# Holding loads back by the bytes in flight: a fused attention and feed-forward kernel

## The chip, the cores and the metric

The kernel runs on one core of a Trainium2 chip. The metric is the device time of one execution in microseconds. One core has five engines with instruction queues of their own: TensorE (PE in the profile; PEld is its weight load), VectorE (DVE), ScalarE (ACT), GpSimd (POOL) and SyncE (SP). GpSimd, SyncE and ScalarE also issue DMAs, which 16 DMA engines carry out.

## The reference

```
B, H, S, D = 8, 12, 448, 64            # q, k, v: [B, H, S, D], float32
scores = q @ k^T / sqrt(D)
attn   = relu(scores)**2 / S
x      = (attn @ v), heads side by side -> [3584, 768]
gate   = relu(x @ w_gate)              # w_gate, w_val: [768, 1536]
val    = x @ w_val
out    = (gate * val) @ w_out          # w_out: [1536, 768]; out: [3584, 768] float32
```

## The kernel before

All inputs are loaded once into SBUF and turned to bf16 by the load itself. The weights stay there: `wg`, `wv` (each 128 x 6 x 1536) and `wo`. Attention goes by quads, four heads of one batch, so there are 24 quads. A quad's k and q go to a `raw` buffer (two of them; the first six quads use space in `gvT`, which is filled with something else later), its two halves of v to a `vv` buffer (three of them; two early quads use `gvT` again). TensorE (the first six quads, L540, L547 and L588) or a copy on VectorE or ScalarE and a DMA transpose from SyncE (the later ones, L612 and L618) turn q and k round into `qkT`. Then come scores (L686), relu and square on ScalarE and VectorE (L697, L699, L709, L711), and the product with v (L728), which leaves x of the batch in `xT`.

The feed-forward part of a batch runs between the quads of later batches. The first two batches multiply with `wg` and `wv` plainly (L793); the others use a scheme with fewer multiplications (L902), and the product with `wo` uses a like one (L1017). Their prepared weights `gvT` and `woT` are made by VectorE from `wg`, `wv` and `wo` (L820, L839). TensorE also gets some filler matmuls in the first 32 us (L1171).

All this is emitted once, without loops on the chip. A planner in the kernel's own Python code merges three written-out orders (`PE_ORDER` for TensorE, `LOAD_ORDER` for the loads, `AHEAD` for VectorE, ScalarE and SyncE) with modelled durations and so fixes the order on every engine. The order on an engine is its queue: an instruction that waits holds back all behind it.

GpSimd issues 117 loads (L404) and does nothing else but four memsets at its start; only the first two pieces of q come from SyncE and ScalarE. A load waits for what its destination needs (that a `raw` or `vv` buffer's last reader is done), and for one of eight DMA semaphores, which the loads take in turn, so for the load eight places before it. Sizes as written in bf16: a q or k load is 224 KB, a v load 112 KB, 256 columns of `wg` or `wv` 384 KB, 128 columns 192 KB, a piece of `wo` 576 KB; the sources are float32, twice that.

Of the kernel before, what the change touches and what calls it, by code (L numbers as in the profile page):

```python
# [9 lines left out]
BF16 = mybir.dt.bfloat16  # L10
# [298 lines left out]
def kernel(  # L309
# [10 lines left out]
    nc = tc.nc  # L320
# [27 lines left out]
    pool = ctx.enter_context(tc.tile_pool(name="sb", bufs=1))  # L348
# [51 lines left out]
    others, pool_ops = [], []  # L400


    def dma_in(dst, src, n_desc, us, deps=(), alloc=(), share=0.25):
        op = Op({"POOL": (0.5 + 0.0004 * n_desc,) * 2}, lambda: nc.gpsimd.dma_start(out=dst(), in_=src),  # L404
                deps=deps, alloc=alloc)
        op.load, op.share = us, share
        pool_ops.append(op)
        return op
# [3 lines left out]
    def load_gv(m0, m1):  # L412

        cols = slice(m0 * 128, m1 * 128)
        for ops, sb, w in ((wg_op, wg, moe_w_gate), (wv_op, wv, moe_w_val)):
            src = w.rearrange("(kd p) f -> p kd f", p=128)
            op = dma_in(lambda sb=sb: sb[:, :, cols], src[:, :, cols], 768,
                        1.075 * (m1 - m0) + (0.0 if wv_op or sb is wv else 0.65))
            for m in range(m0, m1):
                ops[m] = op  # L420

    def load_out(par, hf):
        src = moe_w_out.rearrange("(g par p) m -> p par g m", p=128, par=2)
        wo_op[(par, hf)] = dma_in(lambda: wo[:, par, hf], src[:, par, :, hf * OH:(hf + 1) * OH], 768, 3.0, share=0.19)
# [20 lines left out]
    def first_loads(st, src):  # L445


        n = 4 * QT * D
        wide = hT.rearrange("p k s -> p (k s)").bitcast(FP32)[:, :n].rearrange("p (h t d) -> p h t d", h=4, t=QT)

        def pair(j, eng, queue):
            hs = slice(2 * j, 2 * j + 2)
            k_op = dma_in(lambda: st.raw()[64:128, hs], src(k)[:, hs], 128, 0.05)
            k_op.to = (2.05, None)[j]
            ld = Op({eng: (0.65, 0.65)}, lambda: queue.dma_start(out=wide[0:64, hs], in_=src(q, 0, QT)[:, hs]))
            ld.load, ld.share, ld.hw = 0.1, 0.25, True
            cv = Op({"DVE": (0.46, 0.55)}, lambda: nc.vector.tensor_copy(st.raw()[0:64, hs, :QT], wide[0:64, hs]), deps=[ld])
            cv.kind = "wide"
            others.extend([ld, cv])
            return [k_op, cv]  # L460

        table = Op({"ACT": (1.3, 1.3)}, lambda: None)
        st.qk_ops = [pair(0, "ACT", nc.scalar), pair(1, "SP", nc.sync)]
        table.deps.append(others[-4])
        others.append(table)
        st.load_q = lambda t0, t1: dma_in(lambda: st.raw()[0:64, :, t0:t1], src(q, t0, t1), 256, 0.17 * (t1 - t0))
# [818 lines left out]
```

## Time and profile before

| what | value |
|---|---|
| two runs | 403.55 and 410.82 us, median 407.19 |
| span of the profiled execution | 402.3 us; the nearer run, 403.55 us, is 1.2 us longer |
| TensorE, VectorE, ScalarE, GpSimd busy | 98%, 81%, 68%, 19% |
| mean granted clock of TensorE | 0.990 |
| loads from GpSimd (queue q0) | 23.50 MB, 43.1% of the 16 DMA engines' time |
| stores and transposes (queue q1) | 18.98 MB, 26.5% |
| chain that ended last | PE 95%, DMA 1%, DVE 1% |

The page divides the span into 40 slices of about 10 us and gives for each the busy tenths of every engine, the granted TensorE clock and what the DMA engines moved. The chain that ended last is followed back from the last instruction to what released each. In the view of GpSimd's instructions in order of time, a bracket behind an instruction says how long GpSimd stood idle before it and what ended that. "Landing" is the moment at which a load's semaphore shows that all of it is there.

### The profile page before, as it was taken

Reading aid. Unit: us, or ns where it says so; the run is one execution under the profiler, and the core shown is the slowest. Engines: PE = TensorE matmul, PEld = TensorE weight load, DVE = VectorE, ACT = ScalarE, POOL = GpSimd, SP = SyncE. Lnnn points to the kernel's source line nnn. Section 1 sums busy time; section 2 is a strip of 40 time slices with the busy share of each in tenths; the row PEclk is TensorE's granted clock in tenths of the full one; section 3 lists DMA queues with packets and bytes.
Section 4 is the critical chain, followed back from the end, with each engine's and each line's share of the span. In section 5 each row is a group of like instructions: output and inputs, shape, how many; then the busy total and the mean of one; then the engine's idle time right before and its main releaser. Section 6 shows DMA issues by size and latency. Waiting matters only on the chain.

```text
span 402.3 us, 8737 instructions
## 1 busy us (share of the span) xinstructions
PE 393.8 (98%) x3472; PEld 210.1 (52%) x3472; DVE 326.1 (81%) x568; ACT 274.0 (68%) x399; POOL 75.7 (19%) x121
## 2 busy tenths in 40 slices
PE   6999999999999999999999999999999999999995
PEld 3567745454455554444455554444555555555563
DVE  5688788999989879969988989888789967758662
ACT  3697786477979728969879868878788843333221
POOL 7946441020430110311030221300100000000000
PEclk9799999999999999999999999999999999999999
DMA  8999999948988995193698796682224320000245
GB/s 121 192 198 199 201 193 183 147 48 136 124 144 171 162 116 115 26 145 56 84 141 153 152 131 129 82 92 47 46 37 99 80 59 2 0 0 2 59 118 139
DMA packets 77337, 43.54 MB, mean 108 GB/s; under 512 B 40688, under 2 KB 77296, under 8 KB 77296
## 3 DMA queue, kind: packets, MB, share of 16 engines
q0 software_dynamic: 34640, 23.50, 43.1%
q1 hardware_dynamic: 42192, 18.98, 26.5%
q8 instruction: 27, 0.44, 0.5%
q10 hardware_dynamic: 464, 0.49, 0.4%
q14 instruction: 14, 0.11, 0.1%
HBM read 47.19 MB, written 11.01 MB: 145 GB/s over the span
## 4 chain that ended last, share of the span: by engine, by line
PE 95%; DMA 1%; DVE 1%; POOL 0%; issue 0%; ACT 0%; POOLq 0%
PE ps L902 36%; PE ps L1017 25%; PE ps L793 14%; PE ps L686 10%; PE ps L728 8%; DMA gvT<-in_q_dram 1%; PE ps L1171 1%; PE ps L540 1%; PE ps L588 1%; DVE at L711 1%; POOL gvT L404 0%; DVE at L699 0%; DVE qkT L515 0%; DVE f L853 0%; ACT xT L744 0%
## 5 line engine op out<-in xcount | busy, mean ns | idle before, releaser
L697 ACT ACTIVATE at<-ps 128x896 bf16<-128x896 f32 (+4 forms) x116 | 103.2, 906 | 22.6 <-PE ps L686 21.8
L849 ACT COPY f<-ps 128x448 f32<-128x448 f32 x99 | 52.1, 532 | 45.8 <-PE ps L902 34.2
L709 ACT ACTIVATE at<-at 128x896 bf16<-128x896 bf16 (+1 forms) x72 | 67.0, 947 | 2.0 <-DVE at L699 1.2
L711 DVE TENSOR_TENSOR at<-at 128x896 bf16<-128x896 bf16 (+4 forms) x99 | 58.9, 607 | 9.2 <-ACT at L697 8.1
L699 DVE TENSOR_SCALAR at<-ps 128x896 bf16<-128x896 f32 (+4 forms) x55 | 58.4, 1064 | 6.9 <-PE ps L686 6.2
L404 POOL DMA_DIRECT2D vv<-in_v_dram x44 | 26.7, 611 | 165.5 <-PE ps L686 152.5
L686 PE MATMUL ps<-qkT 64*64 64x448 bf16 (+2 forms) x756 | 51.5, 342 | 1.0 <-ACT xT L744 0.3
L902 PE MATMUL ps<-xT,gvT 128*128 128x448 bf16 x216 | 50.9, 353 | 0.0
L902 PE MATMUL ps<-sx,wv 128*128 128x448 bf16 x216 | 50.6, 353 | 0.1
L902 PE MATMUL ps<-xT,wg 128*128 128x448 bf16 x216 | 49.7, 353 | 0.0
L902 PEld LDWEIGHTS <-gvT 128*128 128x128 bf16 x324 | 30.7, 98 | 30.5 <-issue 3.2
L1017 PEld LDWEIGHTS <-sh 128*128 128x128 bf16 x312 | 29.5, 98 | 22.9 <-issue 3.6
L1017 PEld LDWEIGHTS <-hT 128*128 128x128 bf16 x270 | 25.3, 98 | 20.5 <-issue 4.5
L1017 PE MATMUL ps<-wo,hT 128*128 128x384 bf16 x192 | 35.6, 327 | 0.0
L686 PEld LDWEIGHTS <-qkT 64*64 64x64 bf16 x756 | 19.5, 106 | 27.5 <-issue 22.4
L728 PE MATMUL ps<-at,vv 64*64 64x448 bf16 (+2 forms) x700 | 33.4, 327 | 0.0
L1007 DVE SCALAR_TENSOR_TENSOR o<-ps,f 128x384 f32<-128x384 f32 x41 | 22.5, 554 | 12.1 <-PE ps L1017 7.2
L902 PEld LDWEIGHTS <-wv 128*128 128x128 bf16 x216 | 20.6, 98 | 21.0 <-issue 2.8
L793 PE MATMUL ps<-xT,wv 128*128 128x448 bf16 (+2 forms) x180 | 31.3, 316 | 0.0
L902 PEld LDWEIGHTS <-wg 128*128 128x128 bf16 x216 | 20.6, 98 | 19.9 <-issue 1.7
L851 ACT ACTIVATE f<-ps 128x384 f32<-128x384 f32 x37 | 18.2, 491 | 18.6 <-PE ps L1017 18.3
L793 PE MATMUL ps<-xT,wg 128*128 128x448 bf16 (+2 forms) x180 | 30.6, 315 | 0.0
(72 smaller groups left out, 495.5 us busy)
## 6 DMA issues: line engine op xcount, KB each, us to landing
out_dram<-o SPq DMA_DIRECT2D x108, 96.0 KB, 2.2
vv<-in_v_dram POOLq DMA_DIRECT2D x44, 112.0 KB, 5.1
raw<-in_k_dram POOLq DMA_DIRECT2D x18, 224.0 KB, 5.4
raw<-in_q_dram POOLq DMA_DIRECT2D x18, 224.0 KB, 6.0
wo<-in_moe_w_out_dram POOLq DMA_DIRECT2D x4, 576.0 KB, 16.7
wg<-in_moe_w_gate_dram POOLq DMA_DIRECT2D x5, 384.0 KB, 9.9
wv<-in_moe_w_val_dram POOLq DMA_DIRECT2D x5, 384.0 KB, 10.6
gvT<-in_k_dram POOLq DMA_DIRECT2D x5, 224.0 KB, 6.3
```

The lines of the kernel that those rows point to most:

```text
L404: op = Op({"POOL": (0.5 + 0.0004 * n_desc,) * 2}, lambda: nc.gpsimd.dma_start(out=dst(), in_=src), deps=deps, alloc=alloc)
L686: nc.tensor.matmul(banks()[64 * j:64 * j + 64, z, h2], lhsT=self.k_of(j, h2, k), rhs=self.q_of(j, h2), start=True, stop=True)
L697: nc.scalar.activation(self.at_of(i, m), banks(), AF.Relu)
L699: nc.vector.tensor_scalar_max(self.at_of(i, m), banks(), 0.0)
L709: nc.scalar.activation(a, a, AF.Square)
L711: nc.vector.tensor_tensor(a, a, a, ALU.mult)
L728: nc.tensor.matmul(ps[64 * h2:64 * h2 + 64, ps2.idx + j, :n], lhsT=st.v_of(j, h2, c), rhs=self.at_of(c)[64 * j:64 * j + 64, 0, h2], start= ...
L793: nc.tensor.matmul(ps[:, pb.idx, z * n:(z + 1) * n], lhsT=w[:, kd, fc], rhs=xT_t[xbuf[b].idx][:, kd, cols], start=(kd == 0), stop=(kd == K ...
L849: nc.scalar.copy(dst, src)
L902: nc.tensor.matmul(ps[:, pb.idx, :S], lhsT=w(g)[:, fc], rhs=rhs, start=start and g == 0, stop=stop and g == KH - 1, skip_group_check=True)
L1007: op = Op({"DVE": V384}, lambda: nc.vector.scalar_tensor_tensor(o_t[ob.idx], ps[:, pb.idx, :OH], float(out_scale), f_t[fb.idx][:, :OH], AL ...
L1017: nc.tensor.matmul(ps[:, pb.idx, :OH], lhsT=lhs(kf), rhs=rhs(kf), start=start and kf == 0, stop=kf == FH - 1, skip_group_check=True)
```

## The change

Every load looks back over the loads issued before it, newest first, and adds up their source bytes until 600,000 are reached. If a load lies behind those, and was not looked at before, GpSimd copies one element of its destination into a one-element tile `seen` ahead of issuing the new load. The copy needs the landing of that load, so GpSimd waits for it. 91 such copies stand in the program. The order of the loads, and of the work on the other engines, is the same.

```diff
+    seen = pool.tile([1, 1], BF16, name="seen")
+    issued = []
+    IN_FLIGHT = 600000
+    FLAT = {2: "a b -> a b", 3: "a b c -> a (b c)", 4: "a b c d -> a (b c d)"}
+
     def dma_in(dst, src, n_desc, us, deps=(), alloc=(), share=0.25):
-        op = Op({"POOL": (0.5 + 0.0004 * n_desc,) * 2}, lambda: nc.gpsimd.dma_start(out=dst(), in_=src),
-                deps=deps, alloc=alloc)
+        def emit():
+            d = dst()
+            size = 4
+            for n in src.shape:
+                size *= n
+            held, k = 0, len(issued)
+            while k > 0 and held < IN_FLIGHT:
+                k -= 1
+                held += issued[k][1]
+            if held >= IN_FLIGHT and k > 0 and issued[k - 1][0] is not None:
+                at = tuple(slice(0, 1) for _ in issued[k - 1][0].shape)
+                nc.gpsimd.tensor_copy(seen[0:1, 0:1], issued[k - 1][0][at].rearrange(FLAT[len(at)]))
+                issued[k - 1] = (None, issued[k - 1][1])
+            issued.append((d, size))
+            nc.gpsimd.dma_start(out=d, in_=src)
+
+        op = Op({"POOL": (0.5 + 0.0004 * n_desc,) * 2}, emit, deps=deps, alloc=alloc)
         op.load, op.share = us, share
         pool_ops.append(op)
         return op
```

## The prediction

> **What bounds the kernel now.** I read the first part of the page and its slices, then the stretches of the first 60 us, then GpSimd's own instructions in order of time, because the change touches only what GpSimd issues.
>
> ```profile
> PE 393.8 (98%) x3472; PEld 210.1 (52%) x3472; DVE 326.1 (81%) x568; ACT 274.0 (68%) x399; POOL 75.7 (19%) x121
> PEclk9799999999999999999999999999999999999999
> DMA  8999999948988995193698796682224320000245
> ```
>
> TensorE is busy for 98% of the 402.3 us, so only some 8.5 us could be won at all. The DMA row shows the second resource: for the first fifth of the span the DMA engines are as full as TensorE, and later they are not.
>
> ```profile
> 5.00:10.00 5.00, 3.37 (x67) 1.88 (x65) 2.47 (x5) 2.53 (x4) 3.71 (x7) 0.89 1.18 162
> 10.00:15.00 5.00, 5.00 (x71) 2.71 (x70) 2.79 (x6) 2.11 (x4) 4.66 (x7) 0.50 1.36 197
> 20.00:30.00 10.00, 9.46 (x177) 6.75 (x176) 8.88 (x15) 9.16 (x14) 4.56 (x7) 1.00 1.42 199
> 30.00:40.00 10.00, 9.96 (x189) 7.74 (x186) 8.12 (x14) 7.50 (x14) 5.81 (x9) 1.00 1.38 199
> 40.00:50.00 10.00, 10.00 (x136) 7.26 (x133) 7.58 (x14) 7.25 (x12) 4.97 (x8) 1.00 1.36 201
> ```
>
> After the bounds of the stretch and its length come busy times of PE, PEld, DVE, ACT and POOL, the granted clock, the DMA share and GB/s. From 20 to 50 us loads move at a steady 199 to 201 GB/s (of written bf16 bytes), while TensorE hardly idles. That is a balance: the loads arrive only just ahead of their readers.
>
> ```profile
> 18.12 1.67 POOL L404 DMA_DIRECT2D wg<-in_moe_w_gate_dram  x2
> 21.29 0.84 POOL L404 DMA_DIRECT2D wv<-in_moe_w_val_dram  x1 [0.26 <-DMA wg<-in_moe_w_gate_dram]
> 28.40 0.85 POOL L404 DMA_DIRECT2D wv<-in_moe_w_val_dram  x1 [1.38 <-DMA wg<-in_moe_w_gate_dram]
> 30.96 0.63 POOL L404 DMA_DIRECT2D gvT<-in_k_dram  x1 [1.71 <-DMA wg<-in_moe_w_gate_dram]
> ```
>
> I number the loads from 0 in the order of their issue. The program has eight semaphores for GpSimd's loads, so a load already waits for the one eight places before it. Load 31, at 30.96, waits for load 23 (the second of the pair at 18.12), which landed at 30.68: it took 11.7 us because it stood behind seven others. GpSimd restarts 0.28 us after the landing.
>
> **What the change adds.** 91 of the 117 loads get a one-element copy ahead of them. Nothing is removed, and the order on TensorE, VectorE, ScalarE and SyncE stays. On GpSimd only later loads queue behind a waiting copy, and their readers wait for them. Five VectorE instructions (four at the building of gvT and woT, one late copy at L1069) and one SyncE wait also name a copy; those copies are over long before, so I cost them at nothing. If not, one costs its own lateness once.
>
> The size counts float32 source bytes: a q or k load is 459 KB, a v load 229 KB, 256 columns of wg or wv 786 KB, a piece of wo 1180 KB. So 600 KB means one large weight load, or two of q and k, or three of v, and the next load is issued when the load before those has landed. In place of seven loads ahead there are one to three.
>
> The price of one turn, landing to next landing, has three terms:
> - waking GpSimd: 0.29 us, from the row above and its like;
> - the copy: not in this trace. Nearest rows: the four 128x1 memsets at the start follow each other every 0.03 us, and GpSimd's other kind of instruction, a load's issue, takes 0.59. I take 0.15, as it is nearer to a memset, with one read added;
> - from issue to landing, less the transfer. Load 113, a v load with nothing around it (its group lands in 2.7 us), has 0.57 of transfer, so 2.16. The very first load gives 3.27 - 0.57 = 2.7. A k load at 246.2, beside transposes, gives 4.6 - 1.15 = 3.5; from 10 to 48 us no transposes run. I take 2.3.
>
> One turn is then 0.29 + 0.15 + 2.3 = 2.74 us. Bounds: 2.16 + 0.29 + 0.03 = 2.5 and 2.7 + 0.29 + 0.59 = 3.6.
>
> Transfers, as spacings of landings in the full queue: v 0.57, q or k 1.15, 256 weight columns 1.97 us. With two weight loads in turn, two loads take 2.74 + 1.97 = 4.71 us where they took 3.94; three k loads 2.74 + 1.15 = 3.89 where they took 3.45; four v loads 3.31 where they took 2.28. The full queue becomes one with holes.
>
> Now load by load. A load is issued at its gate's landing + 0.44, or after the issue before it; it lands at max(landing before it, issue + 2.3) + its own spacing of before. Around load 26: load 21 lands at 31.36 instead of 26.15, so load 23, held by it, goes out at 31.80, can start to land at 34.10, where load 22 was done at 33.33 (a hole of 0.77), and lands at 36.66. Load 26 (wv, 128 columns) is held by 23: out at 37.10, ready at 39.40 behind load 25 at 38.41 (a hole of 0.99), landed at 41.17, where it had landed at 34.20. It is 6.97 us late; its matmuls stood at 37.95, so its slack was 3.75.
>
> Where load n lands later than the slack allows, the rest of TensorE's order is moved by the difference. The loads that set this:
> - start: loads 3 and 5, which TensorE waits for now, land at 8.93 and 11.68. Load 5 is needed at 11.72. No loss, with nothing to spare. Load 12 costs the first 0.3 us.
> - load 26: late 6.97, slack 3.75: 3.2 us in all by 38 us.
> - load 35 (wv): lands at 54.8 instead of 45.70, late 9.1, slack 3.75: 5.3 in all.
> - load 37 (wv): late 9.9, slack 4.2: 5.7 in all by 53 us.
> - loads 52 and 53 (the last piece of wo, a q load): late 13.2, slacks 5.2 and 3.7, both of VectorE, which TensorE follows at 88 us after about a microsecond of slack: 8.2 in all.
> - after 92 us GpSimd mostly waits for TensorE, and the page has 152.5 us of such waits. Bursts of three to six loads get 0.5 to 1 us later at their ends; a q load at 141 us without slack loses 0.2. In all 8.4 us.
>
> **The clock.** In the table above TensorE idled 1.6 us between 5 and 10 us, in three pieces and among short transposes, and then the granted clock was 0.50 from 8.9 to 15.7 us. New idle pieces of 2 to 3 us, at 38 and at 88 us, can do the same for 3.4 us or more, which costs half of that, 1.7 us. At 38 us the next late load would swallow it; at 88 us nothing would. I add 1 us, between 0 and 3.4. The Trainium skill (TensorE: Matmul & The Clock Gate, Part 1: The HAM clock gate) says that the clock halves after at least one idle window of about 3.4 us. By that rule no stall of my list is long enough and the term would be nothing; the row shows half speed after less.
>
> **Sum.** The lowest run shown is 403.55 us, which I take for the profiled execution: a span of 402.3 and 1.2 around it. 403.55 + 8.4 + 1.0 = 413 us. The median shown, 407.19, is that of two runs, 403.55 and 410.82, and lies 3.6 above; if the changed kernel's runs spread likewise, its median can be that much higher.
>
> **Rivals.**
> - *The slack swallows most of it.* With the turn at its floor of 2.5 us, the same working gives load 26 about 1.2 us of lateness beyond its slack and 4.3 us in all: 408 us. For it: the quiet v loads at 2.7 to 2.8 us. Against it: weight loads have three times the descriptors and a longer issue (0.85 against 0.60 us).
> - *A slow turn.* If the copy takes as long as an issue, or landing takes the 2.7 of the first load, the turn is 3.1 to 3.6 us and the working gives 14 to 23 us, the clock's share with it: 418 to 427. For it: VectorE is 75 to 90% busy beside the copies, and they are many. Against: issues of GpSimd vary by only 0.1 us beside that VectorE load.
> - *Not slower: a shorter queue lands faster.* If fewer loads in flight make each land sooner, the holes close. The place is the same 10 to 60 us; the working gives no loss at a turn of 2.1 us or less, 0.6 below mine. What could then be won is the idle time before 25 us, some 3.7 us, of which the waits for loads 0 to 5 are about half: 402 to 404 us. Against it: 2.16 from issue to landing was measured with nothing else in flight, and already exceeds 2.1. The Trainium skill (DMA: Bandwidth & Descriptors, Latency and other measured facts) has a lighter HBM load make a DMA's fixed cost smaller, which speaks for this rival; no load of the trace lands faster than the quiet 2.7 us.
> - *The hold doesn't hold*, since eight semaphores already limit the queue: then 403 to 404. Against it: loads now stand seven deep, and each copy waits for the landing of a load two to four places back.
>
> **How the numbers follow.** Forecast (6 to 13 us more) 0.50, slack 0.20, slow turn 0.22, shorter queue 0.06, no hold 0.02. The predicted time is the forecast's, 413. The range goes from 407, below the floor of the turn, to 427, its upper bound; outside are the two last rivals and the far tail. A measurement of this kernel can tell about 2%, some 8 us, from no change. Above that lie the slow turn and 0.8 of the forecast: slower 0.62. Within: the rest of the forecast, the slack and most of the last two: 0.36. Faster: 0.02.
>
> **What would show it.** Right: 91 copies on GpSimd, most of those before 90 us with idle time ahead of them that a DMA ended; loads of wg and wv landing in some 4 to 5 us instead of 10; about 160 GB/s from 20 to 50 us instead of 199 (the 38.3 us of landings from load 4 to 37 become 48); TensorE's busy time unchanged with new idle pieces near 38, 50 and 88 us, ended by DMA or by VectorE; the stretch after 100 us of the same length as before, moved by 8 to 9 us. Wrong: GB/s still near 199 (the turn is short), stalls in the first 12 us (the start has less to spare than I think), copies of 0.5 us or more, or new waits of TensorE after 100 us.

## The result, and the profile after

The changed kernel took 427.39 and 430.85 us, median 429.12, against 407.19 before: a ratio of 1.059 (95% interval 1.043 to 1.075). The ratios, here and below, are estimates from runs outside a slower state that some executions of the chip show, and so are not quite the quotients of the medians. On a second chip, with more runs, the ratio was 1.077 (1.070 to 1.084). The forecast was 413 us with a range to 427; the direction was right, the size was not. In the experiments, on four chips, 62 runs of the kernel before had a median of 403.0 us, so the 403.55 from which the sum was made is the better measure of the two that were shown.

The page's head and slices for the changed kernel:

```profile
PE 403.5 (95%) x3472; PEld 214.3 (50%) x3472; DVE 327.5 (77%) x568; ACT 274.2 (64%) x399; POOL 96.4 (23%) x212
PEclk9579698999899999999999999999999999999999
DMA  7899999999959999718768879775152320000145
```

The DMA digits go no higher than 9 (90% or more) and hide the fall; the GB/s of the stretches show it (columns as in the prediction):

```profile
10.00:20.00 10.00, 7.83 (x121) 4.58 (x117) 5.04 (x12) 4.33 (x7) 5.51 (x14) 0.50 0.87 106
20.00:50.00 30.00, 23.99 (x417) 17.66 (x419) 18.34 (x33) 18.13 (x28) 14.18 (x29) 0.84 1.04 127
```

From 20 to 50 us the loads move 127 GB/s instead of 199, and TensorE works for 24 of the 30 us. GpSimd's own instructions in order of time, from load 19 to load 21:

```profile
26.07 0.82 POOL L423 DMA_DIRECT2D wg<-in_moe_w_gate_dram  x1
29.49 0.18 POOL L420 COPY seen<-wg 1x1 bf16<-1x1 bf16 x1 [2.60 <-DMA wg<-in_moe_w_gate_dram]
29.94 0.82 POOL L423 DMA_DIRECT2D wv<-in_moe_w_val_dram  x1 [0.28 <-issue]
32.50 0.56 POOL L420 COPY seen<-wg 1x1 bf16<-1x1 bf16 x1 [1.75 <-DMA wg<-in_moe_w_gate_dram]
33.01 0.63 POOL L423 DMA_DIRECT2D gvT<-in_q_dram  x1
```

The load at 26.07 landed at 32.38, and the copy at 32.50 answers to that: GpSimd stands still while only one or two loads are under way. Mostly a copy starts 0.12 us after the landing and takes 0.18, as the first one here, and the next load begins some 0.26 us behind it: 0.56 us from landing to issue (the median over the copies that waited is 0.57). TensorE's long idle pieces, in its instructions in order of time:

```profile
47.63 1.14 PE L813 MATMUL ps<-xT,wv 128*128 128x192 bf16 x6 [3.28 <-DMA wv<-in_moe_w_val_dram]
65.67 1.12 PE L813 MATMUL ps<-xT,wv 128*128 128x448 bf16 x5 [3.63 <-DMA wv<-in_moe_w_val_dram]
71.49 1.31 PE L813 MATMUL ps<-xT,wv 128*128 128x448 bf16 x6 [1.05 <-DMA wv<-in_moe_w_val_dram]
109.40 0.38 PE L706 MATMUL ps<-qkT 64*64 64x448 bf16 x2 [1.88 <-DVE hT L823]
```

These are loads 26, 35 and 37 and the wait for VectorE that the prediction named, later than it gave. The chain that ended last says the same: DMA has 14% of the span where it had 1%.

```profile
PE 82%; DMA 14%; POOL 1%; issue 1%; DVE 1%; POOLq 0%; DVEq 0%
```

### The profile page after: what moved, and what is told of

The parts are those of the page before. It is cut to its first block, busy times and chain, and to the rows that moved or that the text cites. A ratio compares the mean times of both kernels' runs of the same rounds, so it can differ in the third digit from the quotient of the medians.

```text
span 425.4 us, 8887 instructions
## 1 busy us (share of the span) xinstructions
PE 403.5 (95%) x3472; PEld 214.3 (50%) x3472; DVE 327.5 (77%) x568; ACT 274.2 (64%) x399; POOL 96.4 (23%) x212
## 4 chain that ended last, share of the span: by engine, by line
PE 82%; DMA 14%; POOL 1%; issue 1%; DVE 1%; POOLq 0%; DVEq 0%
PE ps L922 34%; PE ps L1037 23%; PE ps L813 10%; PE ps L706 8%; PE ps L748 6%; DMA gvT<-in_q_dram 4%; DMA wv<-in_moe_w_val_dram 3%; DMA wg<-in_moe_w_gate_dram 3%; DMA vv<-in_v_dram 2%; DMA gvT<-in_k_dram 1%; DMA raw<-in_q_dram 1%; POOL seen L420 1%; DMA gvT<-in_v_dram 1%; POOL gvT L423 1%; DVE woT L859 0%
## 5 line engine op out<-in xcount | busy, mean ns | idle before, releaser
L719 DVE TENSOR_SCALAR at<-ps 128x896 bf16<-128x896 f32 (+4 forms) x55 | 58.4, 1066 | 12.3 <-PE ps L706 11.9
L706 PE MATMUL ps<-qkT 64*64 64x448 bf16 (+2 forms) x756 | 54.8, 363 | 2.1 <-DVE hT L823 1.9
L922 PEld LDWEIGHTS <-gvT 128*128 128x128 bf16 x324 | 30.7, 98 | 30.4 <-issue 3.1
L813 PE MATMUL ps<-xT,wv 128*128 128x448 bf16 (+2 forms) x180 | 33.2, 328 | 9.3 <-DMA wv<-in_moe_w_val_dram 8.7
L748 PE MATMUL ps<-at,vv 64*64 64x448 bf16 (+2 forms) x700 | 34.8, 337 | 1.1 <-DMA vv<-in_v_dram 1.1
L706 PEld LDWEIGHTS <-qkT 64*64 64x64 bf16 x756 | 20.9, 113 | 29.4 <-issue 25.2
L813 PE MATMUL ps<-xT,wg 128*128 128x448 bf16 (+2 forms) x180 | 32.4, 328 | 0.0
L922 PEld LDWEIGHTS <-wg 128*128 128x128 bf16 x216 | 20.6, 98 | 19.9 <-issue 1.7
```

Source lines behind the costliest of these rows:

```text
L706: nc.tensor.matmul(banks()[64 * j:64 * j + 64, z, h2], lhsT=self.k_of(j, h2, k), rhs=self.q_of(j, h2), start=True, stop=True)
L719: nc.vector.tensor_scalar_max(self.at_of(i, m), banks(), 0.0)
L748: nc.tensor.matmul(ps[64 * h2:64 * h2 + 64, ps2.idx + j, :n], lhsT=st.v_of(j, h2, c), rhs=self.at_of(c)[64 * j:64 * j + 64, 0, h2], start= ...
L813: nc.tensor.matmul(ps[:, pb.idx, z * n:(z + 1) * n], lhsT=w[:, kd, fc], rhs=xT_t[xbuf[b].idx][:, kd, cols], start=(kd == 0), stop=(kd == K ...
L922: nc.tensor.matmul(ps[:, pb.idx, :S], lhsT=w(g)[:, fc], rhs=rhs, start=start and g == 0, stop=stop and g == KH - 1, skip_group_check=True)
```

## The experiments

All are edits of the changed kernel. The ratios are to runs of the kernel before on the same chip.

**Which holds cost.** Three kernels keep the holds of one part of the load order only, by a condition on the load's number; the first is shown, the others have `14 <= len(issued) < 56` and `len(issued) >= 56`.

```diff
-            if held >= IN_FLIGHT and k > 0 and issued[k - 1][0] is not None:
+            if held >= IN_FLIGHT and k > 0 and issued[k - 1][0] is not None and len(issued) < 14:
```

> Holds only ahead of loads 0 to 13. My theory (the price is the length of one turn from landing to next landing, 3.3 us instead of the 2.74 that I had taken, paid where loads arrive just in time): the changed kernel's first 22 us stay as they were there, TensorE 4 to 5 us late by then, and the full queue afterwards makes nothing good: 4 to 6 us over before, 408 to 410 us. Rival A (the start and the half clock that follows it make most of the loss): 12 us or more.

> Holds only ahead of loads 14 to 55. My theory: the start is that of before; load 26 is late by 8 us against a slack of 3.75, load 37 by 18 against 4.2, load 52 by 22 against 5.2: 15 to 18 us over before, 419 to 422 us. Rival A (start): under 12 us.

> Holds only ahead of loads 56 to 116. My theory: GpSimd waits for TensorE there anyway: within 1 us of before. Rival B (every hold costs something, the late bursts too, and half of the holds are here): 5 us or more over before.

Measured: the first 14 loads 1.011 (1.007 to 1.015), some 4.4 us; loads 14 to 55 1.060 (1.055 to 1.064), some 24 us; loads 56 to 116 0.997 (0.993 to 1.001). The start costs what was expected, and rival A falls. The middle costs more than expected, by itself as much as the whole change on its first chip, though less than the 31 us of the second (below). The late holds, 52 of the 91, cost nothing that can be measured, and rival B falls: there GpSimd waits for TensorE anyway.

**The copy without its wait.** The 91 copies stand at their places but read a constant.

```diff
+    fixed = pool.tile([1, 1], BF16, name="fixed")
+    nc.gpsimd.memset(fixed, 1.0)
...
-                nc.gpsimd.tensor_copy(seen[0:1, 0:1], issued[k - 1][0][at].rearrange(FLAT[len(at)]))
+                nc.gpsimd.tensor_copy(seen[0:1, 0:1], fixed[0:1, 0:1])
```

> All 91 copies at their places, but of an element that no load writes, so none of them waits for a landing. My theory: the wait is the price, not the copy; a queue of seven loads hides 0.18 us of copy and the dispatch behind it: within 2 us of before. Rival C (the copies' own time on GpSimd is the price, 91 times 0.18 us and 0.28 us of dispatch, up to 40 of them in the first 90 us): 8 to 16 us over before.

Measured: 1.001 (0.997 to 1.004). From 20 to 50 us this kernel's loads move as much as before:

```profile
20.00:50.00 30.00, 29.93 (x494) 21.95 (x491) 24.41 (x41) 24.26 (x38) 21.33 (x41) 1.00 1.38 199
```

So 91 copies cost nothing as work of GpSimd, and rival C falls. What costs is that the next issue waits for a landing.

**The middle in two parts**, with the changed kernel once more on the same chip; the conditions are `14 <= len(issued) < 46` and `46 <= len(issued) < 56`.

> The changed kernel once more, unaltered, as the measure for the three others on this chip: 22 to 26 us over before.

> Holds only ahead of loads 14 to 45, so wg, wv, q, k and v of the middle, and none ahead of wo. My theory (turns of 3.3 us pile up lateness while the queue is the limit, and the last load short of its slack sets the loss): load 37 is some 18 to 20 us late against a slack of 4.2, and the wo loads add nothing: 13 to 17 us over before. Rival D (the loss is made among the four wo loads, where the end of the loss was seen): under 8 us.

> Holds only ahead of loads 46 to 55 (wo, and the q, k and v among them). My theory: with slacks of 5 us and a transfer of 3 us a load, the lateness stays near the slack: 0 to 3 us over before. Rival D: 8 us or more.

Measured: the changed kernel 1.077 (1.070 to 1.084), some 31 us; loads 14 to 45 1.050 (1.045 to 1.055), some 20 us; loads 46 to 55 1.001 (0.997 to 1.004). The changed kernel and the part to load 45 came out 3 to 5 us above what was expected. Rival D falls, since most of the loss is there without the wo holds. But they cost nothing only by themselves. Matmul by matmul against the trace of before, TensorE is 19.0 us late ahead of its wait at 109.40 us in the changed kernel and 23.5 us late by 115 us; in the second trace of that kernel it goes from 20.8 to 26.3 at the same place, and with the holds of loads 14 to 45 alone it stays at 17.9. So behind a queue that is late already, the wo holds add some 5 us, the half clock behind that wait included.

**The clock.** Matmuls of nothing fill TensorE's stalls ahead of loads 26, 35, 37 and of the scores near 109 us, so that it should not idle there.

```diff
+    done = {"gv": 0, "s": 0}
+    FILL = {("gv", 66): 14, ("gv", 126): 16, ("gv", 138): 5, ("s", 292): 8}
+
+    def fill_at(b, kind, n):
+        one = woT.rearrange("p a f m -> p (a f m)") if kind == "gv" else wg[:, 0]
+        for _ in range(FILL.get((kind, done[kind]), 0)):
+            nc.tensor.matmul(ps[:, b, :S], lhsT=one[:, :128], rhs=one[:, :S], start=True, stop=True)
+        done[kind] += n
...
+                fill_at(ps2.idx, "s", 4 * len(slots))
...
+                        fill_at(pb.idx, "gv", KD)
```

> The changed kernel with 14, 16, 5 and 8 matmuls of nothing put into TensorE's four long stalls (ahead of the first use of loads 26, 35 and 37, and of the scores at 109 us), some 2.6, 3.0, 0.9 and 1.5 us at full clock, so that the clock should stay at 1.0 behind them; their products are overwritten. My theory (late loads set the end, and a slow TensorE between two late loads costs nothing; only the half-speed stretch behind the last stall does): 1 to 3.5 us less than the changed kernel. Rival E (the half clock, 9.7 us of longer matmuls, is a loss of its own): 6 us or more less.

Measured: 1.069 (1.061 to 1.077) beside the 1.077 (1.070 to 1.084) of the changed kernel on the same chip, about 3 us less. The two intervals overlap, so this run does not tell the theories apart. Nor did the fill do all that it was meant to: in its trace, of the slowest of its four runs, TensorE still idles 3.96 us ahead of the scores, which now start at 116.77 us, and is at half speed from 118.0 to 121.4. What speaks against rival E are, weakly, the changed kernel's own runs on two chips: mean clocks of 0.964, 0.967, 0.967, 0.972, 0.974 and 0.980 went with 427, 431, 432, 434, 431 and 435 us. A higher clock did not go with a shorter time. The next experiment says more.

**The dose.** The limit alone is changed.

```diff
-    IN_FLIGHT = 600000
+    IN_FLIGHT = 1200000
```

> The limit at 1,200,000 instead of 600,000 bytes: two large weight loads, three of q or k or six of v ahead of a new one. My theory (a turn of 3.3 us must be covered by the transfers of the loads still in flight): two weight loads cover 3.9 us, so most holes close, and what stays is at the start and behind slow DMA engines: 1 to 8 us over before. Rival F (any hold costs, since the sixteen DMA engines drift apart by 2 to 3 us in the full queue and a hold waits for the last of them): 12 us or more over before.

> The limit at 2,400,000 bytes, three to four large loads ahead. My theory: the transfers in flight cover turn and drift, and the eight semaphores limit nearly as much: within 2 us of before. Rival F: 5 us or more over before.

Measured: 1,200,000 bytes 1.046 (1.040 to 1.053), some 19 us; 2,400,000 bytes 1.002 (0.998 to 1.006). From 20 to 50 us, the first and then the second:

```profile
20.00:50.00 30.00, 27.83 (x499) 20.88 (x494) 23.25 (x40) 22.34 (x36) 15.04 (x30) 1.00 1.22 159
```

```profile
20.00:50.00 30.00, 29.24 (x498) 21.69 (x494) 24.52 (x42) 24.01 (x37) 19.16 (x37) 1.00 1.37 196
```

My theory missed the first badly (1 to 8 us expected) and met the second; rival F met the first and missed the second. Both were wrong as they stood: holds can be free, but only at a depth well beyond what a turn of 3.3 us asks for. At 1,200,000 bytes the mean granted clock was 0.988 to 0.992, beside 0.989 to 1.0 before. The means differ by 0.007, so by estimate some 3 of the 19 us are clock: most of such a loss needs no half clock, against rival E. Not all of it is made by the early loads: in the profiled execution TensorE is 12.3 us late at what had been 92 us, and 5.4 us are added after 200 us.

**A longer turn.** Each copy is written four times.

```diff
+                nc.gpsimd.tensor_copy(seen[0:1, 0:1], issued[k - 1][0][at].rearrange(FLAT[len(at)]))
+                nc.gpsimd.tensor_copy(seen[0:1, 0:1], issued[k - 1][0][at].rearrange(FLAT[len(at)]))
+                nc.gpsimd.tensor_copy(seen[0:1, 0:1], issued[k - 1][0][at].rearrange(FLAT[len(at)]))
```

> The changed kernel with four copies in place of each one, 0.18 us each, so every turn is 0.53 us longer; nothing else moves. My theory: the loss follows the turn, with 14 to 16 us for each us of turn by the working of the prediction: 6 to 12 us over the changed kernel, 430 to 444 us. Rival G (the turn isn't the price, a short queue simply moves fewer bytes per us): under 3 us over the changed kernel.

Measured: 1.097 (1.090 to 1.103), some 39 us over before, against 24 and 31 us for the changed kernel on the two chips: 8 to 15 us more. The time went with the turn, the median from landing to issue went from 0.57 to 1.29 us, and the rate from 20 to 50 us fell from 127 to 111 GB/s:

```profile
20.00:50.00 30.00, 22.40 (x392) 16.73 (x393) 16.96 (x28) 16.65 (x26) 19.79 (x55) 0.83 0.92 111
```

One copy per load cost nothing without a wait; three more behind a wait cost this much. Four without a wait were not run, and the changed kernel was not run on this chip. Rival G falls.

**A load alone.** With a limit of 0, every load waits for the one just before it.

```diff
-    IN_FLIGHT = 600000
+    IN_FLIGHT = 0
```

> Every load waits for the load just before it, so each is alone in its queue and its time from issue to landing can be read. By the prediction's terms (2.3 us and the transfer): 2.9 us for a v load, 3.4 for q or k, 4.3 for 256 weight columns, 5.3 for a piece of wo. By what the changed kernel's trace suggests (2.7 us and more for the wide loads): 2.8, 3.6, 4.7, 5.8. The whole kernel then takes 600 to 700 us, since every load's full turn stands in a row.

Measured, one run: 636.7 us. The view of DMA issues gives the medians from issue to landing, at the end of each line:

```profile
vv<-in_v_dram POOLq DMA_DIRECT2D x44, 112.0 KB, 2.8
gvT<-in_q_dram POOLq DMA_DIRECT2D x3, 224.0 KB, 3.6
gvT<-in_k_dram POOLq DMA_DIRECT2D x5, 224.0 KB, 3.8
wg<-in_moe_w_gate_dram POOLq DMA_DIRECT2D x5, 384.0 KB, 4.7
wo<-in_moe_w_out_dram POOLq DMA_DIRECT2D x4, 576.0 KB, 6.2
```

Less the transfers of the prediction that is 2.2 for a v load, 2.5 to 2.7 for q or k, 2.7 for 256 weight columns and 3.2 for wo (3.0 of transfer). The 2.3 of the prediction holds for narrow loads only; the second set of expected figures is the nearer one.

**The drift of the DMA engines.** A load's semaphore is raised sixteen times, and the trace has each time. From the first to the last raise of one load there are, as the median over loads 14 to 45, 2.5 us in the kernel before, 0.7 in the changed kernel, 1.6 at 1,200,000 and 2.9 at 2,400,000 bytes; with each load alone about 0.5. So the parts of a load in a full queue run apart by one to three microseconds, and the landing is that of the last part. The 2.5 is one execution's figure: where the same loads move at the same 199 or 200 GB/s it is 2.0 with the late holds alone, 2.0 with the holds of loads 46 to 55 alone, and 1.4 with the copies without their wait. A limit between the two tells whether that has to be covered too.

> The limit at 1,800,000 bytes. From 20 to 50 us the loads moved 199 GB/s before, 196 at 2,400,000, 159 at 1,200,000, 127 at 600,000. Theory T (a load's issue to landing as it was alone, 4.6 us for 256 columns, and 0.6 us from landing to the next issue must be covered): 1.8 MB of source are 0.9 MB written, with the new load 1.0 to 1.3 MB, 5 to 6.5 us at 199 GB/s: no loss, within 2 us of before, 190 GB/s or more. Theory H (the DMA engines' drift of 1 to 2.5 us comes on top, since a hold waits for the last of sixteen): 7 us or so must be covered, which 1.8 MB don't: 4 to 10 us over before, 175 to 188 GB/s.

Measured: 1.012 (1.006 to 1.019), some 5 us (2 to 8 by the interval). Theory T said within 2 us, theory H 4 to 10. The rate from 20 to 50 us in the profiled execution, the slowest of its four, is within H's figures:

```profile
20.00:50.00 30.00, 28.06 (x482) 20.92 (x478) 22.75 (x40) 22.39 (x35) 17.45 (x36) 1.00 1.33 183
```

The spread there is 1.8 us. The time lies just outside what T allows, and the rate, of one execution, agrees with H. That supports H against T; it does not show the drift by itself to be the cause, since no run took the drift alone away and a full queue moves as much with a spread of 1.4 us as with 2.5.

**The late holds once more**, as above, with more runs.

> Holds ahead of loads 56 to 116 alone, once more with more rounds, since its first time was a little under that of before (0.997, interval 0.994 to 1.001). My theory: nothing is won, ratio 0.997 to 1.003. Rival (fewer loads beside the transposes make those land sooner): 0.994 or less.

Measured: 0.9966 (0.9936 to 0.9996), just under one and in both expected ranges' reach. Nothing in the profiles shows the late holds to win it: against the shown profile of before, both late-hold profiles run 1.6 to 2.9 us ahead by 24 us, where the programs do the same, and stay within 0.3 us of that to the end. I count it as no gain; a version that clearly beats the kernel before was not found.

## Why the prediction was wrong in size, point by point

**Direction and place: right.** The loss is made by the wait for a landing (the copies alone: 1.001), ahead of what had been 92 us (the late holds: 0.997), and it reaches TensorE through the loads named.

**Lateness less slack: right as a rule.** The load's lateness less its slack of before, beside where TensorE stood against before at its first matmul (VectorE for load 52):

| load | landing before, forecast, after | late less slack | reader late |
|---|---|---|---|
| 26 | 34.20, 41.17, 47.59 | 13.4 - 3.75 = 9.6 | 9.6 |
| 35 | 45.70, 54.8, 65.62 | 19.9 - 3.75 = 16.2 | 16.0 |
| 37 | 48.37, 58.3, 71.45 | 23.1 - 4.2 = 18.9 | 18.75 |
| 52 | 78.29, 91.5, 105.14 | 26.9 - 5.2 = 21.7 | 21.65 |

TensorE follows VectorE at 21.9 us late, and 1.6 us more are the clock's (below). Two readings of the prediction were off by about 1 us each, in opposite directions. VectorE's copy of load 53 stood at 84.78 us, so the slack of that load was 5.35 us and not 3.7; after the change 27.25 - 5.35 = 21.9, and the copy was 22.0 late. And the rule that the prediction states, carried on from load 26, gives 9.7, 10.5 and 14.1 us of lateness for loads 35, 37 and 52, where it has 9.1, 9.9 and 13.2.

**The failing step is the price of one turn**, "0.29 + 0.15 + 2.3 = 2.74 us", and with it "about 160 GB/s", where 127 were moved. Each term was too small:
- Landing to issue was 0.44 and measured 0.56. I had read the 0.28 us between a landing and an issue as a wake-up, to be paid once. A copy wakes in 0.12, and a gap of about 0.26 us then stands between most copies and the issue behind them.
- Issue to landing beyond the transfer was 2.3, taken from one quiet v load. Alone, wide loads have 2.7 to 3.2. "Slow turn", at 0.22, had the 2.7, but from the first load, a narrow one, so by luck; that weight loads have three times the descriptors was said under another rival and not priced.
- A hole was reckoned for the queue as a whole, as if the sixteen parts of a load ended together. They don't. In the changed kernel, with load 18 landed at 29.36 and load 20 issued only at 29.94, the rate sank before load 19 landed:

```profile
28.25:30.50 2.25, 2.25 (x61) 1.71 (x64) 1.39 (x4) 2.17 (x3) 0.74 (x2) 1.00 1.25 164
30.50:32.25 1.75, 1.75 (x46) 1.24 (x39) 1.72 (x3) 1.75 (x4) 0.26 (x1) 1.00 0.59 71
```

Its first part was done at 30.56, its last at 32.38. By the rate, little of load 20 had moved until then, so the parts that were done early had little to do. In the full queue they go on to the next load: before the change, the first part of load 27 was done at 32.09, ahead of the last of load 26 at 34.20. With a turn of 3.3 us the prediction's own working gives some 18 us. Of the rest, 6 to 13 us by chip, 1.6 are the clock's (below); this hole may make the others, but no run shows it apart.

**The start: "no loss, with nothing to spare" was wrong.** Load 5 landed at 12.73 instead of the 11.68 of the forecast and the 11.72 at which it was needed, and loads 12 and 13 at 21.05 and 21.66, where the prediction's working gives 18.35 for load 12. TensorE was 4.8 us late at what had been 22 us, where I had 0.3. Alone this costs 4.4 us (loads 0 to 13). It is the same step: with a turn of 3.3 us the working lands load 5 at 12.5.

**The clock: larger than forecast, its price read in one place only.** The profiled execution has 30.7 us at half speed before its end, 6.8 before the change, and TensorE's busy time rose by 9.7 us. Of these 30.7 us, 17 lie between 9 and 26 us. I had added 1 us, for a stall at 88 us that no late load would swallow. That stall came at 109 us, and behind it the clock was halved for 3.4 us:

```profile
111.48:114.89 3.41, 3.41 (x20) 1.13 (x17) 2.43 (x3) 1.20 (x3) 1.52 (x5) 0.50 1.21 184
```

There TensorE, without a wait, went from 21.9 to 23.5 us late: 1.6 us, where the prediction gave 1.7 for such a piece. Between two late loads a slow TensorE waits less at the second: after half speed from 46.6 to 53.5 us it still stood idle for 3.63 us at load 35. What the half clock of the start costs is open. The row that showed half speed after short idle pieces was the right one to believe: the clock fell at 46.63 us, 2.28 us into the idle piece of 3.28. The Trainium skill (TensorE: Matmul & The Clock Gate, Part 1: The HAM clock gate) names an idle window of about 3.4 us; here less was enough.

**The rivals.** "The slack swallows most" is refuted by 1.059 and more. "Not slower: a shorter queue lands faster" had half a truth: a load of wg lands in 4.7 us instead of 9.9, as the page's line of issues says, and it helped nothing, because the bytes per us fell too. "The hold doesn't hold" is refuted.

```profile
wg<-in_moe_w_gate_dram POOLq DMA_DIRECT2D x5, 384.0 KB, 4.7
```

## What to carry to other kernels

A queue of transfers needs as many bytes in flight as its rate times the time from one issue to the landing that allows the next. Here a wide load's 4.7 us alone and 0.6 us to the next issue, at 199 GB/s, ask for 1.05 MB as written, 2.1 MB of float32 source, as a lowest estimate. Limits of 600 KB gave 127 GB/s, 1.2 MB 159, 1.8 MB 183 and 2.4 MB 196. (A new load comes on top of the limit: at 1.8 MB that makes 1.0 to 1.3 MB as written, and it still cost 5 us.) Latency from issue to landing in a full queue (10 us here) is no measure of harm: check whether the rate is flat and the readers have slack before a queue is made shorter. Where loads arrive just in time, work out lateness less slack load by load; that rule held to a few tenths of a microsecond, and what must be sized with care is the turn, from the slowest kind of load and not the quickest.

## What the runs showed of the hardware that was not expected

- The sixteen raises of one load's semaphore lie 2.5 us apart in the full queue (median, loads 14 to 45; 1.4 to 2.0 in other executions at the same rate), and 0.5 us when the load is alone. A wait for the load is a wait for the last of them.
- A one-element copy on GpSimd takes 0.18 us, at times 0.4 to 1.3, and about 0.26 us pass before the load behind it starts, while two loads follow each other without a gap.
- From issue to landing, less the transfer, a load alone takes 2.2 us at 112 KB and 2.7 at 384 KB, by the line of the load's kind above.
